# Attention and MLP decode kernel: the last K quad in halves, K and V queued in alternation, and the last 64 MLP units on pairs of partitions

## The chip, the cores and the metric

The kernel runs on one core of a Trainium2 chip. Times are device microseconds of that core. The kernel before has a median of 207.77 us over its first 6 runs (207.37 to 208.23), and of 207.82 us over the 20 runs that stood beside the result (207.01 to 208.50). Ratios of two kernels are the mean time of the runs of one over that of the other in the same rounds, so they are not quite the ratio of the medians that are quoted.

The profile's own clock counts from the start of the profiled span, which is a little shorter than the timed run (204.8 us for a run of 206.71).

## The reference

One token of a decoder block: layer norm, attention over a cache of 4,096 positions with 32 heads of 128, projection, residual, layer norm, gated MLP with 1,728 hidden units, residual.

```python
# x: 1 x 640, k_cache and v_cache: 32 x 4096 x 128, all bfloat16
q = (layernorm(x) @ wq).reshape(32, 128)
scores = einsum("hd,hkd->hk", q, k_cache) * 128 ** -0.5
o = einsum("hk,hkd->hd", softmax(scores), v_cache)
h = x + o.reshape(4096) @ wo
n = layernorm(h)
out = h + (gelu(n @ w_gate) * (n @ w_up)) @ w_down     # 640 x 1728, 640 x 1728, 1728 x 640
```

Nearly everything is read once: K and V are 67 MB of the 84 MB.

## The kernel before

Heads are worked in eight "quads" of four. A quad of K is 4 MB, 128 partitions of 32 KB; so is a quad of V. K has two buffers, V has one. VectorE turns K in blocks of 32 by 32, PE makes the scores, ScalarE the exponentials, PE the sum over V ("PV", in two halves of 64 matmuls). SyncE (SP) issues all loads, in program order, on one hardware queue; a wait for a free buffer stands in SP's program ahead of the load.

```python
def load_k(m):
    if m >= SLOTS:                                   # SLOTS = 2
        SP.wait_ge(S["dve"], D_SCORES[m - SLOTS])
    load(f"k{m % SLOTS}", kr[m % SLOTS], rows_of(A_k_cache, m))

def load_v(m):
    dst, src = vt.rearrange("p j d -> p (j d)"), rows_of(A_v_cache, m)
    if m < NQ - 2:
        if m > 0:
            SP.wait_ge(S["pe"], pe_at(m - 1, ("pv", 1)))
        load("va", dst, src)
        SP.sem_inc(S["vb"], 16)
    else:                                            # last two V quads in halves
        for h in range(2):
            SP.wait_ge(S["pe"], pe_at(m - 1, ("pv", h)))
            r = slice(h * TILE // 2, (h + 1) * TILE // 2)
            load(f"v{'ab'[h]}", dst[:, r], src[:, r])
# ...
load_k(0)
for m in range(NQ):                                  # NQ = 8
    if m + 1 < NQ:
        load_k(m + 1)
    load_v(m)
    if m % 2 == 1:
        load_wo(m // 2)
load("wg", wg_sb, B_w_gate.rearrange("(p c) f -> p c f", c=DC))
load("wu", wu_sb, B_w_up.rearrange("(p c) f -> p c f", c=DC))
SP.wait_ge(S["dve"], D_SCORES[NQ - SLOTS])
load("wd0", wd_last, B_w_down[FULL * P : DF, :].rearrange("(p b) d -> p b d", b=PER))
# then wd1, wd2, wd3: rows 0 to 1663 of w_down, 13 per partition, as 8 + 3 + 2
```

So the queue near the end reads K7 (4 MB), V6a, V6b (2 MB each), V7a, V7b, wo, w_gate, w_up, w_down. The last 64 rows of w_down (80 KB, "wd0") lie on partitions 0 to 31, two rows each, and the matching 64 hidden units are computed in one row of PSUM by five matmuls of 64 columns. The y matmuls take the w_down pieces in the order of their landing, wd3 last; then comes one addition and the output.

The softmax here doesn't subtract the row's maximum and nothing guards it: scores larger than these inputs give would overflow.

## Time and profile before

| What | Value | View |
|---|---|---|
| time | 207.77 us median | timed runs |
| time of the profiled run | 206.71 us, span 204.8 | run list |
| PE and DVE busy | 44% and 51% | page, busy times |
| bytes through the queue | 84.2 MB, 96.8% of 16 engines | page, DMA queues |
| chain's end | 22.7 us of w_down load, 8 y matmuls, an addition | chain of waits |

From the page of the kernel before. Each of the 40 characters is a slice of 5.1 us, in tenths of busy time; the row of GB/s is what the 16 transfer engines moved in a slice.

```profile
span 204.8 us, 4115 instructions
...
PE 89.1 (44%) x1856; PEld 54.4 (27%) x1856; DVE 104.9 (51%) x184; ACT 4.6 (2%) x11; POOL 6.8 (3%) x12
...
DMA  7999999999999999999999999999999999999990
GB/s 248 400 472 410 416 467 448 410 410 446 438 435 420 444 416 410 448 442 442 410 398 472 410 442 448 435 416 416 418 446 435 419 426 365 400 428 431 417 376 35
...
q1 hardware_dynamic: 4096, 84.23, 96.8%
```

The transfers are busy from the first slice to the last but one, the compute engines half of the time. The kernel ends when its transfers end. The chain of waits of the same kernel (start, duration, what) agrees:

```profile
178.77 22.68 DMA big<-in_B_w_down_dram
...
201.50 0.34 PE y L362 x8
...
201.86 0.33 DVE y_row L596
```

The last piece of w_down lands at 201.45, and 0.7 us of work follow before the output is written.

The timeline of the kernel before, around the last V quad (start, duration, engine, line, operation; `x64` means merged instructions). The two PV halves of quad 6 and the two loads of V7 that wait for them:

```profile
167.20 1.85 PE L260 MATMUL o<-ex,big 128*128 128x4 bf16 x64 [3.14 <-PEq L167]
169.08 5.22 SPq L431 DMA_DIRECT2D big<-in_A_v_cache_dram  x2
...
172.09 1.85 PE L260 MATMUL o<-ex,big 128*128 128x4 bf16 x64 [3.04 <-PEq L167]
```

V7a goes to the queue at 169.08, once the first PV half has freed its half of the buffer. V7b is the second of the two merged issues and ends at 174.30. At 169.08 the queue holds only what is left of V6b, which lands near 172. The stretches of the trace at that time, and of the end (columns: stretch, its length, busy time and count of PE, PE weight loads, DVE, ACT, POOL, then granted clock, DMA share, GB/s):

```profile
165.00:170.00 5.00, 1.85 (x64) 1.79 (x64) 3.09 (x4) 0.00 (x0) 0.00 (x0) 0.50 0.94 400
170.00:175.00 5.00, 2.34 (x77) 2.20 (x81) 0.67 (x4) 0.00 (x0) 0.00 (x0) 0.50 0.99 380
...
194.00:197.00 3.00, 2.41 (x46) 0.98 (x34) 1.75 (x8) 0.21 (x1) 0.07 (x1) 1.00 1.00 364
```

Most stretches in the middle of the run have 419 to 465 GB/s. The reader is to see two weak places: 165 to 175 us, and 194 to 197 us, where w_up ends and w_down begins.

### The profile page before, as it was taken

How to read it: one execution, taken by the hardware profiler on the slowest of the kernel's cores; microseconds unless marked ns; L12 is line 12 of the kernel's file. 1: busy time of each engine (PE TensorE's matmuls, PEld its weight loads, DVE VectorE, ACT ScalarE, POOL GpSimd, SP SyncE). 2: the span in 40 equal slices, each digit the busy share in tenths (PEclk: the TensorE clock that was granted, in tenths of full speed). 3: DMA queues.
4: the chain of work that ended last, by engine and by line, in shares of the span. 5: the costliest groups of instructions: out<-in, count | busy, mean ns of one | idle time of the engine just before them, and what ended most of it. 6: DMA issues, size and time to landing. Idle time of an engine off the chain costs nothing. (4 is left out here: it accounts for less than half of the span.)

```text
span 204.8 us, 4115 instructions
## 1 busy us (share of the span) xinstructions
PE 89.1 (44%) x1856; PEld 54.4 (27%) x1856; DVE 104.9 (51%) x184; ACT 4.6 (2%) x11; POOL 6.8 (3%) x12
## 2 busy tenths in 40 slices
PE   0003504405643861076407620574166433658963
PEld 0001100115312711073107210531063133217421
DVE  5003399570749468409571874084909480931360
ACT  2000100000000000000000000000000000000000
POOL 8301000000000000000000000000000000000100
PEclk9999955555555555555555755555555555555599
DMA  7999999999999999999999999999999999999990
GB/s 248 400 472 410 416 467 448 410 410 446 438 435 420 444 416 410 448 442 442 410 398 472 410 442 448 435 416 416 418 446 435 419 426 365 400 428 431 417 376 35
DMA packets 4101, 84.30 MB, mean 412 GB/s; under 512 B 480, under 2 KB 480, under 8 KB 768
## 3 DMA queue, kind: packets, MB, share of 16 engines
q1 hardware_dynamic: 4096, 84.23, 96.8%
q8 instruction: 3, 0.05, 0.1%
q14 instruction: 2, 0.02, 0.0%
HBM read 84.23 MB, written 0.00 MB: 411 GB/s over the span
## 5 line engine op out<-in xcount | busy, mean ns | idle before, releaser
L528 DVE STREAM_TRANSPOSE big<-big 128x1024 f32<-128x1024 f32 x64 | 73.8, 1212 | 4.1 <-issue 4.1
L260 PE MATMUL o<-ex,big 128*128 128x4 bf16 x1024 | 28.6, 166 | 41.2 <-PEq L167 41.2
L260 PEld LDWEIGHTS o<-ex,big 128*128 128x128 bf16 x1024 | 28.2, 104 | 41.7 <-issue 41.7
L233 PE MATMUL s<-big,q_quad 128*8 128x512 bf16 x256 | 29.5, 609 | 21.4 <-DVE big L528 21.4
L555 DVE TENSOR_TENSOR o_col<-o,rinv 128x4 bf16<-128x4 f32 x8 | 1.3, 162 | 41.4 <-PE o L260 41.4
L233 PEld LDWEIGHTS s<-big,q_quad 128*8 128x8 bf16 x256 | 7.1, 113 | 38.6 <-DVE big L528 29.6
L537 DVE STREAM_TRANSPOSE s_turned<-s 128x512 f32<-128x512 f32 x8 | 5.7, 717 | 15.1 <-PE s L233 15.1
L266 PE MATMUL a<-wo,o_row 128*1 128x160 bf16 x256 | 9.9, 333 | 2.3 <-DVE o_row L562 2.3
L278 PE MATMUL t<-rs_cur,ones_f 128*128 128x4 f32 x16 | 4.7, 364 | 10.1 <-DVE rs_cur L548 10.1
L540 DVE TENSOR_TENSOR ex<-e,of_head 128x512 bf16<-128x512 f32 x8 | 5.5, 692 | 6.8 <-PE e L248 6.8
L266 PEld LDWEIGHTS a<-wo,o_row 128*1 128x1 bf16 x256 | 7.2, 115 | 3.0 <-DVE o_row L562 3.0
L288 PE MATMUL o<-x_col,mean_f 128*128 128x10 f32 x2 | 0.6, 374 | 16.6 <-DVE x_col L200 16.6
L278 PEld LDWEIGHTS t<-rs_cur,ones_f 128*128 128x128 f32 x16 | 4.0, 311 | 11.0 <-DVE rs_cur L548 11.0
L248 PE MATMUL e<-e_part,ident 128*32 128x32 bf16 x128 | 2.5, 198 | 10.1 <-PEq L326 10.1
L424 POOL TENSOR_TENSOR hr<-hv,half_f 128x1 f32<-128x1 f32 x1 | 0.6, 555 | 174.8 <-DVE hv L208 174.8
L248 PEld LDWEIGHTS e<-e_part,ident 128*32 128x32 bf16 x128 | 1.8, 106 | 16.8 <-issue 16.8
L212 DVE CAST x_row<-x_68 128x160 f32<-128x160 bf16 x1 | 0.2, 245 | 11.6 <-DMA x_68<-in_A_x_dram 11.6
L481 ACT ACTIVATE e_part<-s_turned 128x128 bf16<-128x128 f32 x8 | 2.5, 309 | 155.7 <-DVE s_turned L537 155.7
L353 PE MATMUL s<-ex,ident 128*128 128x512 bf16 x14 | 5.0, 484 | 0.0
L288 PEld LDWEIGHTS o<-x_col,mean_f 128*128 128x128 f32 x2 | 0.5, 313 | 16.6 <-DVE x_col L200 16.6
L281 PE MATMUL o<-col_of,o_spread 128*128 128x8 bf16 x8 | 1.5, 188 | 6.8 <-issue 3.3
L420 POOL MEMSET wo<- 128x5120 bf16 x1 | 4.4, 4370 | 0.0
(79 smaller groups left out, 43.4 us busy)
## 6 DMA issues: line engine op xcount, KB each, us to landing
big<-in_A_k_cache_dram SPq DMA_DIRECT2D x8, 4096.0 KB, 20.6
big<-in_A_v_cache_dram SPq DMA_DIRECT2D x6, 4096.0 KB, 17.6
big<-in_A_v_cache_dram SPq DMA_DIRECT2D x4, 2048.0 KB, 12.1
big<-in_A_wq_dram SPq DMA_DIRECT2D x1, 5120.0 KB, 15.4
wo<-in_A_wo_dram SPq DMA_DIRECT2D x4, 1280.0 KB, 15.6
big<-in_B_w_gate_dram SPq DMA_DIRECT2D x1, 2160.0 KB, 14.3
big<-in_B_w_up_dram SPq DMA_DIRECT2D x1, 2160.0 KB, 19.4
big<-in_B_w_down_dram SPq DMA_DIRECT2D x1, 1280.0 KB, 21.7
```

What stands on the lines that cost most here:

```text
L233: inst = PE.matmul(s_bank[32 * r : 32 * r + 2 * QH, :], lhsT=q_quad[:, 2 * k + e, (1 - b) * QH : (3 - b) * QH], rhs=kt_at[:, k, HALF * b + ...
L248: inst = PE.matmul(to[32 * h : 32 * h + 32, r], lhsT=ident[:, 32 * r : 32 * r + 32], rhs=e_part[:, :, :, h], start=True, stop=True, tile_p ...
L260: inst = PE.matmul(o_ps, lhsT=vt[:, j, :], rhs=e_t[:, j, :], start=(j == 0), stop=(j == NB - 1))
L266: inst = PE.matmul(attn_ps[32 * r : 32 * r + 1, :], lhsT=o_row[:, j : j + 1], rhs=wo_t[:, j, r * YW : (r + 1) * YW], start=False, stop=j = ...
L278: mark("totals", PE.matmul(ps, lhsT=ones_f[:], rhs=rs_cur[:], start=True, stop=True))
L281: inst = PE.matmul(ps, lhsT=o_spread[:].rearrange("p h c -> p (h c)"), rhs=col_of[:], start=True, stop=True)
L353: PE.matmul(s_bank[:], lhsT=ident[:], rhs=e_t[:].rearrange("p j h -> p (j h)"), start=True, stop=True)
L420: POOL.memset(t[:], 0.0).then_inc(S["pool"], 1)
L481: ACT.activation(e_part[:].rearrange("p b j h -> p j b h"), s_turned[:, :, 0 : 2 * QH].rearrange("p j (b h) -> p j b h", b=2), AF.Exp, sca ...
L528: DVE.transpose(to[:, c], of[:, c].rearrange("p (j k n) -> p j k n", k=2, n=HP)).then_inc(S["kt"], 1)
L537: assert dve(lambda: DVE.transpose(s_turned[:].rearrange("p j n -> p (j n)"), s_bank[:]), False) == D_SCORES[m]
L540: DVE.tensor_tensor(e_t[:], e_ps.unsqueeze(2).broadcast_to(shape), of_head[:].unsqueeze(1).broadcast_to(shape), op=ALU.mult,).then_inc(S[" ...
```

## The change

The intent: fewer stalls at the end of the attention stage, and less small work in the MLP. The last K quad is loaded in halves, and the queue becomes K7a, V6a, V6b, K7b, V7a, V7b. The last 64 hidden units are computed in all four PSUM rows, doubled on pairs of partitions; a mask of zeros and ones keeps each unit for one half of the output columns on the even partition and for the other half on the odd one. So wd0 is now 128 partitions of 640 bytes. Gate and up matmuls write PSUM in an order that lets one transpose serve for all 480 columns.

```diff
+    def load_last_k(half):
+        if half == 0:
+            SP.wait_ge(S["dve"], D_SCORES[NQ - 1 - SLOTS])
+        r = slice(half * TILE // 2, (half + 1) * TILE // 2)
+        load(f"k1{'b' if half else ''}", kr[1][:, r], rows_of(A_k_cache, NQ - 1)[:, r])
 ...
-        if m + 1 < NQ:
+        if m + 1 < NQ - 1:
             load_k(m + 1)
+        else:
+            load_last_k(m + 2 - NQ)
         load_v(m)
 ... turn_keys waits for the second half of the last quad too
-    load("wd0", wd_last, B_w_down[FULL * P : DF, :].rearrange("(p b) d -> p b d", b=PER))
+    load("wd0", wd_last, B_w_down[FULL * P : DF, :].rearrange("i (b d) -> (i b) d", b=PER))
 ... up(): 4 matmuls of 64 columns per chunk for 1, PSUM written with a stride
+                        rhs = w[:, j, r * RG : (r + 1) * RG].rearrange("p (n c) -> p n c", c=FULL)
+                        to = row[:, 0:RG].rearrange("q (c n) -> q n c", c=FULL)
 ...
-    fill(4)
-    end("u", up(u_ps, wu_sb, {0: "wu"}))
-    fill(4)
+    fill(10)
+    end("u", up(u_ps, wu_sb, "wu"))
+    fill(3)
 ... turn_rows: one transpose of 480 columns for two
-        for c, n, at in ((0, FULL, 0), (FULL, PER, RG)):
-            rows = ps[:, at : at + HP * n].rearrange("q (p c) -> q c p", c=n)
-            dve(lambda: DVE.transpose(col[:, c : c + n, :], rows), False)
+        dve(lambda: DVE.transpose(col[:].rearrange("p c n -> p (c n)"), ps), False)
 ...
-    dve(lambda: DVE.tensor_scalar(g_sb[:], g_sb[:], hr[:], None, op0=ALU.mult))
+    dve(lambda: DVE.scalar_tensor_tensor(g_sb[:], g_sb[:], hr[:], units[:], op0=ALU.mult, op1=ALU.mult))
```

## The prediction

> **What bounds the kernel now.** The transfers. In the slices of the page, the DMA share stands at 0.9 or more from slice 2 to the last but one while PE is busy 44% and DVE 51% of the 204.8 us span. The queue table has 84.2 MB, 96.8% of the 16 engines' time. The chain of waits ends with 22.7 us of the w_down load, then eight y matmuls (0.34 us), the last add (0.33 us) and the output. So a change pays only if it makes the queue of transfers end sooner.
>
> The five-microsecond windows show 419 to 450 GB/s through the middle and two weak stretches late: 165 to 175 us (400 and 380 GB/s) and the end. The packet records of the trace (steady: 16,384 bytes in 611 ns, 430 GB/s in all) sharpen this. From 171 to 173 us only 12 to 15 engines work, and packets take 1,100 to 1,500 ns: 239, then 294 GB/s, a loss of (191+136)/430 = 0.76 us. From 177 to 180 us the rate is 389 to 410: 0.2 us lost. The cause is in the timeline: the first half of the last V quad waits for the first PV half of quad 6 (end 169.05), which waited for V6's first half, which stands in the queue behind the 4 MB of K7. V7's first half is issued with only 3 us of work queued, V7's second half at 174 us with little more. [...]
>
> **What the change does.**
> 1. Queue order becomes K7a, V6a, V6b, K7b, V7a, V7b. V6a lands about 4.9 us sooner (2 MB at 430 GB/s), near 162; PV half 0 of quad 6 ends near 166 (its exponentials are ready at 163), PV half 1 near 169. K7b needs no new wait. So V7a is issued with about 6 us queued, V7b with 8 or more: the hole at 171 us and the weakness at 177 us vanish. Worth 0.7 to 1.0 us, all on the critical path.
> 2. K7's second half lands near 172 instead of 162, but before it was transposed only from 174.6 on: now 172 to 176.6, so quad 7's scores, PV and projection come about 2.5 us sooner. Slack, not time: gate, up and down still wait for weights.
> 3. The 64 last units: 40 matmuls for gate and up instead of 25 (small ones), y 56 for 60, one transpose of 480 columns in place of two (0.75 us to about 0.7), one product with the mask. Before, hid was ready at 198.7 and y waited until 199.6 for w_down: a saving here is hidden. The 10 filler matmuls (2.6 us at full clock) end near 195, about when w_up lands; up is done by 197.
> 4. The 80 KB load: 128 packets of 640 bytes for 32 of 2,560. From 102 ns (2,560) and 149 ns (3,840) I estimate 31 ns, 8 per engine: +0.05 us. The slump at 195 to 198 us (0.45 us), where w_down begins, stays.
>
> **Sum.** -1.0 + 0.05: near -1.0 us. **206.7 us**, range 205.9 to 207.5. Faster over 2%: 1%; within 2%: 98%; slower over 2%: 1%.
>
> **What would show it.** Right: no dry engines near 171 us, V7a issued near 166, w_down landed near 200.5 us, wait of u for w_up short or none, y still released by w_down. Wrong: a new hole elsewhere; y released by hid.
>
> **What would upset it.** The end spread of engines (mean 1 us before the last) changing; fillers at half clock holding up u; small packets slower than estimated.

## The result

The changed kernel takes 205.82 us (median of 10 runs, 205.65 to 206.05), the kernel before beside it 207.82 us (20 runs, 207.01 to 208.50). The ratio is 0.991, interval 0.9896 to 0.9923: within 2%, as predicted, but the gain is 2.0 us where 1.0 was forecast, and the median lies just under the low end of the range (205.9). The runs also lie closer together: 0.4 us from lowest to highest, against 1.5 us before.

From the page of the changed kernel:

```profile
span 204.1 us, 4179 instructions
...
PE 90.2 (44%) x1887; PEld 55.1 (27%) x1887; DVE 105.2 (52%) x184; ACT 4.6 (2%) x11; POOL 6.8 (3%) x12
...
DMA  7999999999998999999989999999999999999990
GB/s 249 401 474 411 411 443 482 411 411 409 456 446 379 482 430 418 411 430 475 424 378 489 418 418 418 443 463 418 395 428 424 443 418 424 443 422 429 414 367 20
...
q1 hardware_dynamic: 4336, 84.23, 96.7%
```

Its chain of waits still ends on w_down, landed at 200.71 us:

```profile
173.95 26.75 DMA big<-in_B_w_down_dram
...
200.75 0.34 PE y L367 x8
...
201.11 0.33 DVE y_row L620
```

The timeline around the last V quad, and the same stretches:

```profile
163.13 1.85 PE L265 MATMUL o<-ex,big 128*128 128x4 bf16 x64
165.01 4.51 SPq L448 DMA_DIRECT2D big<-in_A_v_cache_dram  x2
...
167.32 1.84 PE L265 MATMUL o<-ex,big 128*128 128x4 bf16 x64 [2.34 <-PEq L170]
```

```profile
165.00:170.00 5.00, 2.11 (x69) 1.97 (x73) 2.59 (x6) 0.00 (x0) 0.00 (x0) 0.50 1.02 433
170.00:175.00 5.00, 2.87 (x48) 1.37 (x48) 2.79 (x3) 0.00 (x0) 0.00 (x0) 0.50 0.99 423
...
194.00:197.00 3.00, 3.00 (x37) 1.19 (x38) 1.99 (x10) 0.22 (x1) 0.00 (x0) 1.00 0.99 410
```

V7a is issued at 165.01, four microseconds sooner, with V6b and K7b still queued. The weak place at 165 to 175 us is gone (433 and 423 GB/s for 400 and 380). But so is the one at 194 to 197 us (410 for 364), which the prediction said would stay. And the landing of w_down in these two profiles is only 0.74 us apart, while the timed runs are 2.0 us apart. These two things needed explaining.

### The profile page after: what moved, and what is told of

It reads as the page before. It is cut to its first block, busy times and chain, and to the rows that moved or that the text cites. A ratio compares the mean times of both kernels' runs of the same rounds, so it can differ in the third digit from the quotient of the medians.

```text
span 204.1 us, 4179 instructions
## 1 busy us (share of the span) xinstructions
PE 90.2 (44%) x1887; PEld 55.1 (27%) x1887; DVE 105.2 (52%) x184; ACT 4.6 (2%) x11; POOL 6.8 (3%) x12
## 5 line engine op out<-in xcount | busy, mean ns | idle before, releaser
L238 PE MATMUL s<-big,q_quad 128*8 128x512 bf16 x256 | 27.9, 579 | 23.9 <-DVE big L554 23.9
L293 PE MATMUL o<-x_col,mean_f 128*128 128x10 f32 x2 | 0.6, 376 | 16.5 <-DVE x_col L205 16.5
L358 PE MATMUL s<-ex,ident 128*128 128x512 bf16 x19 | 6.1, 457 | 0.0
L293 PEld LDWEIGHTS o<-x_col,mean_f 128*128 128x128 f32 x2 | 0.5, 310 | 16.5 <-DVE x_col L205 16.5
```

The source lines that it names most:

```text
L238: inst = PE.matmul(s_bank[32 * r : 32 * r + 2 * QH, :], lhsT=q_quad[:, 2 * k + e, (1 - b) * QH : (3 - b) * QH], rhs=kt_at[:, k, HALF * b + ...
L358: PE.matmul(s_bank[:], lhsT=ident[:], rhs=e_t[:].rearrange("p j h -> p (j h)"), start=True, stop=True)
```

## The experiments

Besides the views of the profile, I used the trace's records of single transfer packets. In a steady stretch a packet of 16,384 bytes takes 611 ns on its engine, one of 17,280 takes 644 and one of 10,240 takes 385, so 16 engines move about 430 GB/s. For a stretch I add, over all engines, the idle time and the time above these values, and divide by 16: "lost per engine". In the trace's own time the last w_down packet of the kernel before ends at 201.01 and its landing is recorded at 201.45; the difference is 0.43 to 0.45 us in four other profiles too. Packet times below are given 0.44 us later than the trace has them, so that they compare with landings. The packets do not name their engine; an engine was followed by letting each packet start where another ended, which can confuse two engines in step. Sums over all engines do not depend on it. When each engine ended its share of a load is read without this: in the trace the semaphore of a load over 128 partitions gets sixteen updates, which I take as one from each engine, and "landed" is the last of them.

| Run | lost per engine, 170 to 183 us | lost per engine, 192 to 197.6 us |
|---|---|---|
| before, the profiled run of 206.71 us | 1.0 | 0.4 |
| after | 0.0 | 0.0 |

### Each part alone

The order alone is the diff above without its MLP lines; the MLP part alone is the changed kernel with `load_last_k` taken out again:

```diff
 # order alone, from the kernel before
-        if m + 1 < NQ:
+        if m + 1 < NQ - 1:
             load_k(m + 1)
+        else:
+            load_last_k(m + 2 - NQ)
 ... load_last_k itself and the wait in turn_keys as above
```

> The kernel before with only the last K quad in halves and K and V alternating. Theory H (the hole): the whole gain of the change comes from the engines no longer running dry at 171 us, so this alone gives 205.8 to 206.0 us, and its runs spread by less than 0.6 us as those of the changed kernel do. Rival M (the MLP part and the new shape of the 80 KB load, which took away the weak stretch at 195 us): this gives 206.4 to 207.0 us.

> The changed kernel with the K and V order of before put back. Theory H: 207.6 to 207.9 us, with the spread of before (over 1 us between runs). Rival M: 206.8 to 207.3 us.

With the kernel before at 207.98 us: the order alone took 206.23 us (206.14 to 206.38, ratio 0.9929, interval 0.9894 to 0.9963); the MLP part alone took 207.91 us (207.49 to 208.41, ratio 1.0013, interval 0.9977 to 1.0050). The order carries most of the gain, and the narrow spread too. The MLP part alone gains nothing that can be seen, though its packet records show the weak place at 194 us gone (0.0 us lost per engine). So neither theory is right as it stood: the order explains 1.75 us, and 0.4 us of the whole change are left over. The interval of the MLP part alone reaches down to 0.9977, a gain of 0.5 us, so it is not shown that the MLP part gains only when the hole is gone.

To read that last share from one chip, both were run again:

> The order alone once more, on the same chip as the whole change, to read the share of the MLP part from one job. If the layout of the 80 KB load is worth what the weak stretch lost (0.5 us of each engine's time): 206.2 to 206.4 us here, 0.4 to 0.5 us over the whole change. If the 0.4 us between the two jobs was a difference of chips: the same as the whole change within 0.15 us.

> The whole change, same job: 205.8 us, its runs within 0.5 us of each other.

The order alone took 206.22 us (206.19 to 206.35), the whole change 205.85 us (205.67 to 206.08), the kernel before 207.88 us. No run of the one is as fast as any run of the other. The split of the gain is 1.66 us for the order and 0.37 us for the MLP part on top of it.

### The hole filled in another way

K stays whole here. Part of the gate weights, which have a buffer of their own and wait for nothing, goes ahead of V7a:

```diff
+        if m == NQ - 1:
+            load("wg", wg_sb[:, 0:3], wg_rows[:, 0:3])
         load_v(m)
 ...
-    load("wg", wg_sb, B_w_gate.rearrange("(p c) f -> p c f", c=DC))
+    load("wg2", wg_sb[:, 3:DC], wg_rows[:, 3:DC])
```

> The kernel before, K in whole quads, but three of the five chunks of the gate weights (1.3 MB, 3.1 us at 430 GB/s) are queued ahead of the last V quad, so that the engines have work at 171 us. Same bytes, same last K. Theory H: as the order alone, 205.8 to 206.2 us, no dry engines at 171 us. If it is not the hole but the earlier quad 7 that matters: no gain, 207.8 us.

It took 206.36 us (206.17 to 206.53, ratio 0.9934, interval 0.9899 to 0.9969): the gain of the order alone, nearly to the last tenth. Its stretches:

```profile
165.00:170.00 5.00, 1.85 (x64) 1.79 (x64) 3.26 (x4) 0.00 (x0) 0.00 (x0) 0.50 0.97 414
170.00:175.00 5.00, 2.15 (x73) 2.01 (x77) 0.47 (x4) 0.00 (x0) 0.00 (x0) 0.50 1.01 431
...
194.00:197.00 3.00, 2.79 (x45) 1.18 (x38) 1.86 (x8) 0.21 (x1) 0.27 (x1) 1.00 0.96 371
```

Quad 7 runs no sooner here than before (its PV starts at 184.58 us, before at 184.38), and still 1.6 us are gained. What counts is that the queue holds work while the V buffer is waited for. It need not be K.

### The hole made larger

```diff
-            SP.wait_ge(S["pe"], pe_at(m - 1, ("pv", h)))
+            SP.wait_ge(S["pe"], pe_at(m - 1, ("pv", 1 if m == NQ - 1 else h)))
```

> The kernel before with the first half of the last V quad waiting for the second PV half of quad 6 instead of the first: it is issued near 174 us instead of 169. A larger dose of the suspected cause. Theory H: the engines are dry from 171.5 to about 176.3 us, 4 us more than before, so 211.5 to 212 us. If some of a hole is given back because it lets the lagging engines catch up before the end: 210.5 to 211.3 us.

It took 211.37 us (211.00 to 212.06), 3.4 us more than before, which falls between the two forecasts. The stretch from 170 to 175 us moved 16 GB/s. V7a was issued at 174.12. But the time does not settle what was asked: the chain of its profiled run (212.06 us, the slowest of the six) no longer ends on a transfer.

```profile
176.98 24.32 DMA big<-in_B_w_up_dram
...
201.34 2.16 PE u L379 x16
203.50 1.82 PE s L353 x4
205.32 1.90 PE y L362 x51
```

After w_up landed, the up matmuls, four fillers and 51 y matmuls ran one behind the other; in the kernel before, the y matmuls waited for w_down instead. So a large hole costs what it starves, but part of these 3.4 us belongs to PE work that is hidden in the other kernels. Whether lagging engines catch up can be read from the semaphore updates of this run: the engines end V6b spread over 2.2 us (169.95 to 172.11) and V7a within 0.7 us (180.92 to 181.61). They do catch up in a large hole.

### The kernel before, profiled again

> The kernel before, unchanged, profiled again: its profile on hand fell on an execution of 206.71 us, faster than nearly all its timed runs (207.0 to 208.5). If the hole costs a varying amount, an execution near 207.8 us shows more lost at 171 to 181 us, or engines that end later than 202.3 us, by about 1 us.

> The same once more: time at the end of the last w_down packet and mean end of the engines are to be compared with the time of the run.

The two took 207.88 and 208.43 us (single runs; both lie within the runs of the kernel before). The ends of their chains:

```profile
179.17 23.45 DMA big<-in_B_w_down_dram
...
203.15 0.32 DVE y_row L596
```

```profile
179.14 24.15 DMA big<-in_B_w_down_dram
...
203.70 0.33 DVE y_row L596
```

| Profiled run | time | w_down landed | lost per engine, 170 to 183 us |
|---|---|---|---|
| before | 206.71 | 201.45 | 1.0 |
| before, again | 207.88 | 202.62 | 1.2 |
| before, once more | 208.43 | 203.29 | 1.4 |
| order alone | 206.26 | 201.02 | 0.0 |
| after | 205.83 | 200.71 | 0.0 |

In the three runs of the kernel before, the loss per engine grows by 0.4 us, but the landing moves by 1.8 us. The time follows the landing: it is 5.1 to 5.3 us behind it in all five rows. And the landing is that of the last engine. In the run of 208.43 us, thirteen engines have ended w_down by 201.1, then come three at 201.5, 202.1 and 203.3. In the run of 206.71 us, thirteen end by 200.8 and three between 201.42 and 201.45. The difference is there as soon as the hole is over: V7a lands at 177.52, 178.61 and 179.37 us in the three runs, also 1.8 us apart, though V6b landed at 171.95, 171.98 and 172.11. So the hole takes about a microsecond from an engine on average, but hits single engines harder: the packet records of the two slower runs show an engine that gets its first packet of V7a 1.7 to 1.9 us after its last of V6b, while others have no gap at all. The whole transfer waits for the unluckiest engine. The profile that the prediction was made from had a lucky one.

### What the weak place at 194 us was

Three kernels, all from the order alone:

```diff
 # wide: same bytes, the new shape (wrong on purpose: nothing else is changed to fit it)
+    load("wd0", part(FULL * D, D // 2), B_w_down[FULL * P : DF, :].rearrange("i (b d) -> (i b) d", b=2))
 # early: the old shape and line, moved ahead of the load of w_up
 # every fourth partition: the old 32 packets of 2,560 bytes (wrong on purpose)
+    load("wd0", part(FULL * D, PER * D)[0:P:4], B_w_down[FULL * P : DF, :].rearrange("(p b) d -> p (b d)", b=PER))
```

> The order-alone kernel (206.23 us) with one thing of the MLP part added: the 80 KB of w_down go to 128 partitions in packets of 640 bytes instead of 32 partitions in packets of 2,560 (the result is wrong on purpose, the arithmetic is left as before). Theory L (the layout of this load makes the weak stretch at 194 to 197 us): 205.8 us, as the whole change, and the stretch is gone from the packet records. Rival C (the missing 0.4 us comes from the fewer transposes and y matmuls or the clock): 206.2 us.

> The order-alone kernel with the 80 KB load, in its old shape, queued ahead of w_up instead of behind it. Correct result. Theory L: the weak stretch follows the load to about 189 to 191 us, none at 195, and the time stays near 206.2 us. Rival W (the strided rows of the rest of w_down are slow to start): the weak stretch stays at 195 us.

> The order-alone kernel with the 80 KB still in 32 packets of 2,560 bytes, but landing on every fourth partition from 0 to 124 instead of on partitions 0 to 31 (wrong result on purpose). If it is the crowding on 32 neighbouring partitions that slows everybody: weak stretch gone, 205.8 us. If it is the source or the packet size: weak stretch stays, 206.2 us.

| Kernel | median (range) of 6 runs | ratio to before, with interval |
|---|---|---|
| wide | 205.99 (205.83 to 206.25) | 0.9918 (0.9881 to 0.9955) |
| early | 206.50 (206.37 to 206.59) | 0.9941 (0.9905 to 0.9978) |
| every fourth partition | 205.92 (205.82 to 206.18) | 0.9915 (0.9879 to 0.9952) |

The intervals overlap, because the runs of the kernel before spread by 2 us. The kernels' own runs do not: every run of the early load is slower than every run of the other two. The order alone was not run in this job; against its 206.22 and 206.23 us in two other jobs, the two wrong kernels gain 0.2 to 0.3 us. The stretches where the load falls, first of the order alone, then of the early one, then of the two others:

```profile
194.00:197.00 3.00, 1.22 (x24) 0.63 (x25) 0.71 (x4) 0.00 (x0) 0.00 (x0) 0.91 0.95 364
```

```profile
188.00:191.00 3.00, 3.00 (x12) 1.16 (x15) 1.76 (x8) 0.00 (x0) 0.00 (x0) 0.50 0.99 345
194.00:197.00 3.00, 0.77 (x22) 0.45 (x23) 1.00 (x5) 0.21 (x1) 0.00 (x0) 1.00 0.99 415
```

```profile
194.00:197.00 3.00, 1.45 (x27) 0.77 (x28) 1.17 (x6) 0.00 (x0) 0.00 (x0) 1.00 0.98 408
```

```profile
194.00:197.00 3.00, 1.48 (x27) 0.77 (x28) 1.80 (x10) 0.21 (x1) 0.00 (x0) 1.00 0.98 411
```

The weak place goes with the 80 KB: moved ahead of w_up, it stands at 188 to 191 us (345 GB/s) and is gone from 194 us. There it slowed packets of w_up from 644 to about 820 ns (the worst took 1,024), though these have nothing to do with w_down. And it is not the packet's size, nor the source rows: 32 packets of 2,560 bytes on every fourth partition do no harm (411 GB/s). What does harm is that all 32 land on partitions 0 to 31: that is all that differs between the order alone (364 GB/s) and the last of the three kernels.

The harm is not confined to the small load: the packets of w_up beside it are slowed too (the 644 to about 820 ns above). By what the loads get in each other's way no run here shows.

(Both wrong kernels passed the comparison with the reference. The 64 units out of 1,728 weigh too little to be noticed there, so that comparison would not have caught a mistake in this load.)

### An attempt at the engines that end late

In the changed kernel, by the packet records, twelve engines finish w_down between 198.5 and 199.0 and four between 200.0 and 200.7, as if 1.5 us could still be won. The last load was cut with the aim that one engine gets none of it:

```diff
 ... wd1 and wd2 as before; PE waits for wd3 and wd4
+    load("wd3", wd_sb[0:120, a:b, :], wd_rows[0:120, a:b, :])
+    load("wd4", wd_sb[120:P, a:b, :], wd_rows[120:P, a:b, :])
```

> The changed kernel with its last w_down load (128 rows of 2,560 bytes) cut in 120 rows and 8 rows. [...] It tells where the late engines of the end are: if the spared engine is one of those that end near 201.4, the end comes no later and the spared one ends 0.8 us sooner; if not, the end comes 0.0 to 0.1 us later: 205.8 to 205.9 us.

It took 207.00 us (206.81 to 207.43), 1.2 us more than the changed kernel; the expectation (205.8 to 205.9) failed. From 198.2 us on, its packets of 2,560 bytes took about 205 ns instead of 102, for 1.6 us. Four engines still ended late. In the trace the two loads have 15 and 8 semaphore updates at their landing, after one at the issue, where a load over 128 partitions has sixteen; whether an engine was spared, and which, no view shows. Why the packets took twice as long was not shown either.

Where the four late engines come from is settled only in part. In the changed kernel one engine is late from the first load on (1.2 us behind the eighth to finish; the load of wq landed at 16.5 us), and nothing says why. Three more, 0.9, 1.5 and 1.7 us behind, appear between 45.6 and 65.5 us, and up to the last V load the four lags then stay the same within 0.03 us, so none catches up. In the stretch where they appear the records show three packets on the queues that the page calls "instruction": two of 16,384 bytes at 50.5 and 56.7 us, which took 1,091 and 1,099 ns, and one of 8,192 bytes at 50.5 us, which took 307 ns. The data packet after each was slow too (1,681 ns after the large ones and 1,748 after the small one, in place of 1,215). An engine that fetches a large one is then about 1.6 us behind (1.09 + 0.47), one that fetches the small one about 0.8 us (0.31 + 0.53). Three fetches, three newly late engines, and delays of about the right size. Two more fetches follow, a small one at 191.2 us, after which the largest lag grows from 1.7 to 1.9 us, and a large one at 198.9 us, after which none grows. The run with the enlarged hole fits as well: there the hole levels the lags, the next small fetch comes at 196.7 us, and one engine alone ends w_down late, 1.1 us behind the others. But the records do not name the engines, and no run took the fetches away.

## Why the prediction was right or wrong

**That the transfers bound the kernel: right.** In all kernels but the one with the enlarged hole, the chain ends on a wait for w_down.

**The hole, its cause, and that the new order removes it: right.** V7a is issued at 165.0 (foretold: near 166), no engine runs dry, and another filling of the hole (the gate weights first) gains the same 1.6 us. One reading in it was off: its times of packets are 1.3 us later than the trace's own, so the 3 us of work that it saw queued at V7a's issue were too many. In the trace's time the first engine ended V6b at 169.56, 0.5 us after that issue began (169.08), and the first packet of V7a started at 170.03, 0.95 us after it.

**The worth of the hole, "0.7 to 1.0 us, all on the critical path": too small.** It measured 1.66 us. The term was the average over the 16 engines, and it was read from one profile and taken off the median of other runs. The end is set by the last engine, and the profile was of a run of 206.71 us, below all 20 timed runs of the kernel before that stood beside the result (later, 8 of 33 runs were below 207.0). In that run the order alone would have gained only 206.71 - 206.22 = 0.5 us, in the run of 208.43 it would have gained 2.2 us. The warning was there: a profiled run that lies outside the range of the timed ones. The landing of w_down was foretold near 200.5 and came at 200.71, but that is partly luck: the order alone brings it to 201.02, and the rest is the MLP part, which the prediction had at a cost of 0.05 us.

**"The slump at 195 to 198 us, where w_down begins, stays": wrong.** I took it for a property of w_down's rows. It was the 32-partition load of 80 KB, which I had costed as a load of its own (+0.05 us for the smaller packets) and not as a neighbour of others. The small packets did take what was estimated (32 ns measured, 31 estimated). The MLP part, which spreads them over 128 partitions, was worth 0.37 us on top of the order; 0.2 to 0.3 us of it came with the spread load alone, and what the rest comes from was not tested.

**Quad 7 about 2.5 us sooner, and worth nothing: right.** Its PV begins at 182.05 instead of 184.38, and the run with the gate weights first gains the same without it.

**The MLP work hidden: right, but its cost was missed.** I called the added matmuls small. The groups of up matmuls of the kernel before and of the changed one, by shape (busy time, mean ns of one):

```profile
L379 PE MATMUL u<-big,hc 128*1 128x416 bf16 x20 | 1.2, 339 | 0.6 <-DMA big<-in_B_w_up_dram 0.6
```

```profile
L392 PE MATMUL u<-big,hc 128*1 128x416 bf16 x20 | 2.0, 512 | 0.0
```

Both ran at full granted clock (1.00), on the same 416 columns, and one went from 339 to 512 ns. What differs is that the changed kernel writes its PSUM row with a step of 32 values, and that it has 40 up matmuls for 25. No run separates the two. So up ended at 197.7 where 197 was foretold. It did not cost time here: hid was ready at 198.7 and y still waited for w_down.

## What to carry to other kernels

When a kernel is bound by one queue of loads, look at what is queued at the moment when the issuer waits for a buffer: put loads that need no wait ahead of that wait, so that the engines never see the wait (worth 1.6 to 1.75 us here). Value such a hole by the engine that ends last, over several executions, and be wary of a profile whose own run is faster than all timed ones. And spread even a small load over the partitions: on 32 neighbouring ones it slowed the large loads around it (364 GB/s where 408 to 411 were reached with it spread).

## What else was measured here

- In the trace's time and on a drained queue (kernel before and enlarged hole), the first packets of V7a started 0.95 and 0.96 us after the issuing instruction began, 0.62 and 0.63 us after it ended.
- Transfers restarted slowly after the engines ran dry: in the kernel before most first packets of V7a took 1,100 to 1,500 ns instead of 611, and with the idle time an engine lost 1.0 to 1.4 us on average.
- One load on few partitions slowed other loads in flight: packets of 17,280 bytes went from 644 to about 820 ns beside the 80 KB load on partitions 0 to 31.
- In the changed kernel packets of 16,384 bytes on the queue called "instruction" took 1.1 us each, the data packet that followed the two at 50.5 and 56.7 us took 1,681 ns instead of 1,215, and the engines that fell behind at that time were still behind at the last V load, by the same lags within 0.03 us.
